# Zero products on TensorE ahead of the first scores

## The chip, the cores and the metric

The kernel runs on one core of a Trainium2 chip. A core has five engines that run side by side and meet through semaphores: TensorE (PE, matrix products; its weight loads are listed as PEld), VectorE (DVE), ScalarE (ACT), GpSimdE (POOL) and SyncE (SP), which only issues loads and stores to the DMA engines. The metric is the device time of one execution in microseconds (us), the median of several runs. A profile is one execution; its times count from the start of the span.

## The reference

Two layers follow each other. The first is attention with a window of 32 positions on either side, for 8 batch entries, 8 heads, 576 positions and 64 elements per head:

```python
scores = scale * np.matmul(q, k.transpose(0, 1, 3, 2))
mask = np.abs(pos[:, None] - pos[None, :]) <= window
attn = np.exp(scores - scores.max(-1)) / sum        # masked scores count as zero
attn_out = np.matmul(attn, v)                       # to x: [8, 576, 512]
```

The second is a causal attention with 4 experts, each position weighted over its best two:

```python
logits = x @ w_gate                                 # 4 experts
for e in range(4):
    q, k, v = x @ wq[e], x @ wk[e], x @ wv[e]       # 64 wide
    ye = causal_softmax(scale * q @ k.T) @ v @ wo[e]
    out += gate[e] * ye                             # gate: softmax over the best two, else 0
```

Inputs and outputs are float32.

## The kernel before

**Tiling.** The work goes through the 8 batch entries. In the first layer each entry has two groups of four heads. `sc(b, g, half, ...)` makes the scores of one group and one half of the queries: 80 products in the profile's count, 32 rows by 64 columns of the array each, in float32. Two such steps fill the four PSUM tiles `PS[0]` to `PS[3]` (each 128 partitions by two halves of 512 float32 elements). `ex` takes the exponential on ACT, `mk` multiplies by the mask on POOL or DVE, `av` multiplies by v on PE, `un` normalises on DVE, `xt`, `xf` and `xb` turn the result into the layout of the second layer. Its steps (`ga` to `gu` for the gate, `pp`, `pv` for projections, `ps` for scores, `po` for the product with v, `py` for the output) are woven in between.

**What sets the order.** `ORDER` is a list written out by hand, one word per step; `name@banks` says which PSUM halves the step uses. The loop at the end of the kernel runs through the list once and emits each step's instructions, so that every engine has its instructions in the list's order, and each waits by semaphore for what it needs. The dependencies come from the tile framework. All engine calls also go through a recording wrapper, `Watched`, whose `note` compares the boxes of two accesses and declares them independent if no box is common. All engine instructions therefore have line 146 in the profile. For PSUM tiles the wrapper's `boxes` widens each access to all 128 partitions and to whole halves of a tile.

```python
if b.tensor.name.startswith("PS"):
    p0, n, lo, hi = 0, 128, 2 * lo // row, (2 * hi - 1) // row + 1
    row = 2
```

**The head of the program.** The first words of the list are `fk01 fq01 fk11 s_pads fk00 s_warm gq01 s_ones fq10 fq00 fq11 gk00 ...`, and after them the first score steps, `sc001`, `sc000`, `sc011`, `sc010` (batch entry, group, half).
- `fk` and `fq` issue the first loads of k and q, half a group each, on the queues of SP and ACT.
- `gk` and `gq` transpose what has arrived from `kn`, `qn` into `Tkn`, `Tqn`, on DVE, two instructions each. `tk` and `tq` are the same for a whole group, later.
- `s_pads` clears the padding of eleven tiles and WG, on DVE. `s_ones` clears 2 x 32 columns of each half of each PSUM tile in partitions 64 to 127 (one instruction per tile), so that what the score products don't write is defined, and sets the ones next to v. `s_warm` loads ACT's table.
- `load`, used for all further loads, makes a load wait for the latest product emitted so far (`PACE`), so that loads follow the work.

```python
for t in PS:
    nc.vector.memset(t[64:128, :, 0:512].rearrange("p a (c x) -> p a c x", x=256)[:, :, :, 0:32], 0.0)
for t in VSB:
    nc.vector.memset(t[:, :, :, 64:66], 1.0)
```

DVE's order in the head is thus: clears of `s_pads`, transposes of `gq01`, the four PSUM clears and two clears of V, then the transposes of `gk00`, `gk01` and the others.

## Time and profile before

| What | Value |
|---|---|
| Time, median of 3 runs | 252.1 us (250.35 to 256.52) |
| Span of the profiled execution | 248.2 us |
| PE busy | 211.8 us (85% of the span) |
| DVE busy | 182.7 us (74%) |
| ACT busy | 151.3 us (61%) |
| POOL busy | 148.5 us (60%) |
| First product on PE | 10.77 us |
| Four score steps, in two pairs of 160 products | 10.77 to 15.23 us and 16.50 to 21.03 us |

The busy shares are averages over the whole span. The stretch that the change touches is the first 10 us, in which PE has nothing to do, and what follows from it. Lines of the timeline give start, time from start to end of a merged group, engine, line, operation, what is written and read, the count, and in brackets the idle time before it and what ended it. The clock that PE was granted (PEclk) is in tenths of full speed on the page and as a fraction in the table of stretches.

### The profile page before, as it was taken

How to read it: one execution, taken by the hardware profiler on the slowest of the kernel's cores; microseconds unless marked ns; L12 is line 12 of the kernel's file. 1: busy time of each engine (PE TensorE's matmuls, PEld its weight loads, DVE VectorE, ACT ScalarE, POOL GpSimd, SP SyncE). 2: the span in 40 equal slices, each digit the busy share in tenths (PEclk: the TensorE clock that was granted, in tenths of full speed). 3: DMA queues.
4: the chain of work that ended last, by engine and by line, in shares of the span. 5: the costliest groups of instructions: out<-in, count | busy, mean ns of one | idle time of the engine just before them, and what ended most of it. 6: DMA issues, size and time to landing. Idle time of an engine off the chain costs nothing.

```text
span 248.2 us, 12156 instructions
## 1 busy us (share of the span) xinstructions
PE 211.8 (85%) x5453; PEld 170.8 (69%) x5466; DVE 182.7 (74%) x373; ACT 151.3 (61%) x230; POOL 148.5 (60%) x164
## 2 busy tenths in 40 slices
PE   0277787999999869999579994999999999999981
PEld 0276774787879648886449864788789777887550
DVE  7986958699888967887827792889686654727770
ACT  2037656488678557768444782666674868492952
POOL 6038779338994997449971696048959488240310
PEclk9999997999999999999979998899999999999997
DMA  6968849676878995779975788034890061656045
GB/s 235 300 180 231 192 110 257 170 212 216 190 206 240 192 231 133 203 218 210 246 230 156 199 191 193 22 100 132 163 222 15 16 186 41 54 194 222 13 184 211
DMA packets 64787, 42.93 MB, mean 173 GB/s; under 512 B 54752, under 2 KB 55776, under 8 KB 64736
## 3 DMA queue, kind: packets, MB, share of 16 engines
q1 hardware_dynamic: 64080, 40.91, 64.7%
q10 hardware_dynamic: 656, 1.25, 1.4%
q8 instruction: 43, 0.70, 1.2%
q14 instruction: 8, 0.07, 0.1%
HBM read 30.42 MB, written 9.44 MB: 161 GB/s over the span
## 4 chain that ended last, share of the span: by engine, by line
PE 70%; DMA 12%; DVE 9%; issue 3%; ACT 3%; SPq 1%; ACTq 0%; DVEq 0%
PE PS L146 70%; DMA OTT<-OE 8%; DMA kn<-in_k_dram 2%; DVE XTB L146 2%; DMA V<-in_v_dram 1%; DVE Tkn L146 1%; ACT ATE L146 1%; DVE PS L146 1%; ACT Y L146 1%; DVE OE L146 1%; DVE Y L146 1%; ACT A L146 1%; DVE XTF L146 0%; DVE m L146 0%; ACT V L146 0%
## 5 line engine op out<-in xcount | busy, mean ns | idle before, releaser
L146 POOL TENSOR_TENSOR A<-A,MASKP 128x576 f32<-128x576 f32 x62 | 87.0, 1425 | 39.1 <-ACT A L146 39.1
L146 ACT ACTIVATE ATE<-PS 128x1024 bf16<-128x1024 f32 (+1 forms) x64 | 51.0, 835 | 23.6 <-PE PS L146 20.6
L146 PE MATMUL PS<-Tqn,Tkn 32*64 32x128 f32 (+2 forms) x2560 | 47.2, 276 | 15.8 <-DVE Tqn L146 11.3
L146 ACT ACTIVATE A<-PS 128x576 f32<-128x576 f32 x64 | 38.6, 650 | 34.2 <-PE PS L146 28.2
L146 PEld LDWEIGHTS PS<-Tqn,Tkn 32*64 32x64 f32 x2560 | 41.6, 141 | 21.6 <-DVE Tqn L146 11.7
L146 POOL TENSOR_SCALAR_AFFINE_SELECT ATE<-ATE 128x512 bf16<-128x512 bf16 (+1 forms) x48 | 24.7, 528 | 29.7 <-ACT ATE L146 29.6
L146 PE MATMUL PS<-V,A 128*64 128x65 f32 (+1 forms) x1280 | 40.9, 228 | 1.3 <-ACT V L146 0.8
L146 PEld LDWEIGHTS PS<-V,A 128*64 128x64 f32 (+1 forms) x1280 | 37.7, 137 | 5.1 <-issue 2.6
L146 DVE STREAM_TRANSPOSE Tkn<-kn 128x576 f32<-128x576 f32 (+1 forms) x36 | 37.3, 1122 | 3.9 <-DMA kn<-in_k_dram 2.6
L146 DVE STREAM_TRANSPOSE Tqn<-qn 128x576 f32<-128x576 f32 (+1 forms) x36 | 37.3, 1120 | 2.1 <-DMA qn<-in_q_dram 2.1
L146 PE MATMUL PS<-WO,OTT 128*128 128x512 bf16 (+1 forms) x83 | 18.9, 345 | 11.5 <-DMA OTT<-OE 9.2
L146 DVE TENSOR_TENSOR XN<-PS,RC 128x512 f32<-128x512 f32 (+1 forms) x40 | 25.5, 638 | 1.4
L146 POOL COPY V<-V 64x1024 f32<-64x1024 f32 (+1 forms) x22 | 21.8, 992 | 5.3 <-issue 2.5
L146 ACT COPY Y<-PS 128x1024 f32<-128x1024 f32 (+1 forms) x18 | 15.0, 842 | 14.6 <-PE PS L146 10.7
L146 PE MATMUL PS<-XTB,WQ 128*128 128x288 bf16 x128 | 19.5, 304 | 1.8 <-DVE XTB L146 1.8
L146 PE MATMUL PS<-ident,XN 128*128 128x128 f32 x144 | 19.2, 277 | 0.7 <-issue 0.7
L146 POOL CAST XTB<-XTF 128x128 bf16<-128x128 f32 (+1 forms) x18 | 11.4, 647 | 13.6 <-ACT XTF L146 12.9
L146 PE MATMUL PS<-WV,XTB 128*128 128x256 bf16 (+1 forms) x192 | 18.6, 256 | 0.8 <-ACT A L146 0.4
L146 ACT COPY XTF<-PS 128x1024 f32<-128x1024 f32 (+1 forms) x26 | 16.5, 679 | 4.4 <-PE PS L146 3.7
L146 PE MATMUL PS<-XTB,WK 128*128 128x288 bf16 x128 | 18.9, 296 | 0.0
L146 PEld LDWEIGHTS <-OTT 128*128 128x128 bf16 (+1 forms) x96 | 6.9, 101 | 17.2 <-DMA OTT<-OE 9.7
L146 PEld LDWEIGHTS <-ATE 128*128 128x128 bf16 x480 | 16.5, 97 | 2.0 <-issue 0.8
(62 smaller groups left out, 247.7 us busy)
## 6 DMA issues: line engine op xcount, KB each, us to landing
V<-in_v_dram SPq DMA_DIRECT2D x32, 256.0 KB, 4.0
out_dram<-Y SPq DMA_DIRECT2D x16, 512.0 KB, 3.1
kn<-in_k_dram SPq DMA_DIRECT2D x14, 576.0 KB, 5.1
qn<-in_q_dram SPq DMA_DIRECT2D x14, 576.0 KB, 5.1
kn<-in_k_dram SPq DMA_DIRECT2D x4, 288.0 KB, 5.2
qn<-in_q_dram ACTq DMA_DIRECT2D x4, 288.0 KB, 5.6
V<-in_v_dram SPq DMA_DIRECT2D x8, 128.0 KB, 4.7
out_dram<-Y SPq DMA_DIRECT2D x15, 64.0 KB, 2.0
```

What stands on the lines that cost most here:

```text
L146: return lambda *a, **k: self._w.note(self._e, f(*a, **k))
```

## The change

Ahead of everything, a small tile `WZ` of 128 x 224 bf16 zeros is cleared on DVE, and TensorE multiplies zeros by zeros 72 times into a part of `PS[3]` that nobody reads before it is written again (second half, columns 288 to 511). The products have no use but to keep TensorE occupied while the first loads are under way, so that its clock[...] is up when the first scores come. Everything else in the list stands as it was.

```diff
 ORDER = """
-    fk01 fq01 fk11 s_pads fk00 s_warm gq01 s_ones fq10 fq00 fq11 gk00 ...
+    s_wm fk01 fq01 fk11 s_pads fk00 s_warm gq01 s_ones fq10 fq00 fq11 gk00 ...
@@
+    WZ = sb.tile([128, 224], BF16, name="WZ")
@@
+    def s_wm():
+
+        for i in range(72):
+            nc.tensor.matmul(PS[3][:, 1, 288:512], WZ[:, 0:128], WZ, start=True, stop=True)
@@
     with tc.manual_schedule():
+        nc.vector.memset(WZ, 0.0)
         nc.vector.memset(RC[0], 0.0)
         for step in ORDER.split():
```

The products are emitted through `nc.tensor.matmul`, not through the kernel's `mm`, so they don't count as the latest product for `load`.

## The prediction

> **What bounds the kernel now.** I read the chain that ended last first. It gives TensorE (PE) 70% of the span, but that is an average over stages. So I asked for the same chain in the first 30 us, where the change sits (columns: start us, us, what):

> ```profile
> 0.81 0.40 SPq L350
> ...
> 1.72 6.09 DMA kn<-in_k_dram
> 7.82 0.02 issue
> 7.84 2.34 DVE Tkn L146 x4
> 10.18 0.55 DVE Tqn L146
> 10.73 0.04 issue
> 10.77 4.46 PE PS L146 x139
> ```

> The head is a load, then VectorE (DVE), then PE. The load ends at 7.8 us, five transposes on DVE take 2.9 us, and only then can the first scores start. PE is empty until 10.77 us, but PE is not what is short there. The timeline of DVE and PE over the head and, in its last row, later (start us, us, engine, line, operation, count):

> ```profile
> 0.88 0.07 DVE L146 MEMSET RC<- 128x8 f32 x1 [0.88 <-PEq L672]
> ...
> 6.66 0.59 DVE L146 MEMSET PS<- 64x128 f32 x4
> 7.27 0.31 DVE L146 MEMSET V<- 128x128 f32 x2
> 7.84 2.34 DVE L146 STREAM_TRANSPOSE Tkn<-kn 128x288 f32<-128x288 f32 x4 [0.27 <-DMA kn<-in_k_dram]
> ...
> 10.77 4.45 PE L146 MATMUL PS<-Tqn,Tkn 32*64 32x64 f32 x160 [10.77 <-DVE Tqn L146]
> ...
> 16.50 4.53 PE L146 MATMUL PS<-Tqn,Tkn 32*64 32x64 f32 x176 [1.28 <-ACT A L146]
> ...
> 53.18 2.43 PE L146 MATMUL PS<-Tqn,Tkn 32*64 32x64 f32 x160
> ```

> DVE has 0.27 us of slack before the first k transpose; it is otherwise busy from 0.88 to 17.7 us without a break. And the same 160 score products take 4.45 us at 10.77 but 2.43 us at 53.18: the first four score steps run at half the clock. The page's clock row says 9 there, because the record begins with the first change it saw, near 20 us; the pace of the products is the witness. That is the 2 us per pair that the change is after.

> When the clock falls again is seen in stretches that I cut around idle times (stretch, length, busy times and counts of the engines, PEclk, DMA share, GB/s):

> ```profile
> 40.40:44.00 3.60, 3.55 (x16) 2.29 (x16) 2.94 (x13) 0.84 (x3) 3.40 (x3) 0.53 0.92 298
> 44.00:46.00 2.00, 2.00 (x18) 1.52 (x16) 1.61 (x2) 0.64 (x1) 1.44 (x2) 1.00 0.01 5
> 89.70:91.70 2.00, 0.00 (x0) 0.11 (x2) 1.24 (x3) 0.43 (x1) 2.00 (x2) 1.00 0.71 206
> 91.70:95.20 3.50, 3.45 (x96) 2.63 (x96) 2.15 (x3) 2.19 (x4) 2.34 (x3) 1.00 0.21 78
> 122.40:125.40 3.00, 0.00 (x0) 0.11 (x2) 0.55 (x1) 0.07 (x1) 2.33 (x3) 1.00 1.26 210
> 125.40:129.20 3.80, 3.75 (x44) 2.08 (x47) 0.76 (x1) 1.89 (x3) 2.78 (x3) 0.57 0.82 286
> 149.80:153.10 3.30, 0.06 (x2) 0.00 (x0) 1.18 (x3) 0.47 (x1) 3.01 (x4) 1.00 1.07 142
> 153.10:156.60 3.50, 3.40 (x62) 3.41 (x64) 0.90 (x2) 0.37 (x1) 0.00 (x0) 0.52 0.41 143
> ```

> An idle PE of 2.0 us keeps the clock; idle times of 3.0 and 3.3 us are each followed by about 3.4 us at half speed.

> [...] half-speed spells last 3.4 us and end in busy stretches. [...] products with N = 288 start every 240 ns cold and 121 ns warm, those with N = 256 every 108 ns. [...]

> **The change, part by part.**

> A `memset` of WZ (128 x 112 words) goes first on DVE. By the rows of XTB (two of 128 x 128 words in 0.31 us) it takes about 0.15 us. It delays the other clears by that, and 0.27 us of slack before the k transposes swallows it.

> The 72 products start at about 0.88 + 0.15 + 0.05 = 1.1 us on an empty PE. N is 224. Cold, 224 x 240/288 = 187 ns each; warm, 121 - 64 x (121 - 108)/32 = 95 ns by the trace's slope[...]. Their weight loads (98 ns warm, 152 cold in the rows of N = 288) lie under the products. [...]
> - Early release: 18 cold products (3.4 us) and 54 warm (5.2 us) end at 9.7 us.
> - Late release: 36 cold (6.8 us) and 36 warm (3.5 us) end at 11.4 us.
> - Middle: 10.5 us.

> If this were all, the stretch would end just as the first scores begin (10.77 us), warm.

> But it adds a wait. The products write the second half of the last PSUM tile, PS[3], columns 288 to 511. `s_ones` later clears columns 0 to 31 and 256 to 287 of each PSUM half. No element is shared, but the helper that declares independence, `Watched.boxes`, rounds every PSUM access to whole halves of a tile, so the clear of PS[3] is held to clash. In the built order of the changed kernel, DVE's fourth PSUM clear waits for a PE count of 72, which the last product alone raises. Queued behind it on DVE are the two clears of V, then all the transposes of q and k; the first scores wait for the first five of those. That clear ran at 7.09 us (the last 0.165 us of the 0.59). Now it runs when product 72 is complete: 10.5 + 0.17 (rest of its 0.26 us) + 0.05 = 10.75 us, between 9.9 and 11.6. Then 0.17 + 0.31 us of clears, and the k transposes start at 11.2 us instead of 7.84: **+3.4 us** (2.6 to 4.3). The scores start at 11.2 + 2.93 = 14.2 us.

> Does the warm clock pay it back? Between the last product and the first score PE idles 0.05 + 0.48 + 2.93 = 3.5 us, longer than both idle times above after which the clock fell. So the usual outcome is a clock that is back at half before the first score, and the four score steps run as slowly as now. The loads paced by products (`load`) move along with PE; those not paced (k and V issued by 7.83 us) land earlier against the work, for which I give 0.3 us back. Nothing downstream is anchored to anything else: scores, exponentials, masks and later loads all hang on these transposes. Sum: 252.1 + 3.4 - 0.3 = **255.2 us**.

> **The rivals.**
> - *The clock survives the gap* (18%). [...] Then both score pairs take about 2.4 us, 4.1 us less PE time. But DVE's own chain stays late: the second pair needs the second group's transposes, done at 15.5 us now and 18.9 us then. What comes back is bounded by DVE's 1.41 us wait for q before 19.14 us: about 1.7 of the 3.4. 252.1 + 1.7 = 253.8 us.
> - *Zeros never release the clock* (10%). 72 x 187 ns end at 14.6 us, the clear runs at 14.8, the transposes start at 15.3: +7.4, 259.5 us. [...] no row of this trace shows zero operands.
> - *Faster* (8%): the stretch is warm from its start, 72 x 96 ns end at 8.0 us, the wait costs 1.2 us, and the scores give back 4.1: 249.2 us. Against it: PE is cold at 10.77 us now after doing nothing.
> - *As worked out* (64%).

> **How the numbers follow.** The likeliest case gives 255.2. The three times before span 250.35 to 256.52, and full or half clock after later idle times (three further falls within the span, 1.7 us each at most) is drawn anew, so each case carries about 1.5 us either way. From 252.0 (below the surviving clock, less noise) to 259.0 us (main case at its late end, 256.1, plus noise, and short of the middle of the zero case) leaves out about 2 in 10. Slower by over 2% means above 257.1 us: nearly all of the zero case and a tenth or more of the main one, 0.19. Faster by over 2% (below 247.0 us) needs the fast case with luck, 0.03. Within 2%: 0.78.

> **What would show it.** The fourth PSUM clear on DVE should wait on PE until about 10.7 us, with the k transposes right after at 11.2; if it runs near 7 us, my wait is wrong. Starts of the 72 products should go from 187 to about 96 ns apart between 4.5 and 7.9 us; 187 to the end is the zero case. First scores at 13.3 to 15.1 us, the first 160 in about 4.4 us; if in 2.4, the clock survived. A first score near 10.8 us would overturn the forecast, as would a head late by 3.4 us whose lateness is gone by 60 us.

## The result, and the profile after

The changed kernel takes 267.6 us (265.2 to 272.8) beside 251.2 us of the kernel before (four runs each): a ratio of 1.073, 95% interval 1.051 to 1.095. The forecast was 255.2 us, at most 259.0; it had the direction and missed most of the size. The time of the kernel before spreads from 242 to 258 us over all its runs, so everything below is compared by ratios to runs of it made beside each kernel, and a ratio takes only those runs of a kernel that lie within 1.5% of its fastest (times are medians of all). The profile below is of the execution of 272.8 us.

The timeline of the head, after the change (start us, us, engine, line, operation, count, and in brackets what ended the idle time before it):

```profile
1.11 9.93 PE L146 MATMUL PS<-WZ 128*128 128x224 bf16 x72 [1.11 <-DVE RC L146]
...
6.78 0.45 DVE L146 MEMSET PS<- 64x128 f32 x3
...
11.15 0.17 DVE L146 MEMSET PS<- 64x128 f32 x1 [3.92 <-PE PS L146]
...
11.56 2.27 DVE L146 STREAM_TRANSPOSE Tkn<-kn 128x288 f32<-128x288 f32 x4
...
14.42 3.81 PE L146 MATMUL PS<-Tqn,Tkn 32*64 32x64 f32 x160 [3.38 <-DVE Tqn L146]
...
19.51 1.96 PE L146 MATMUL PS<-Tqn,Tkn 32*64 32x64 f32 x119 [1.28 <-ACT A L146]
...
24.16 3.24 PE L146 MATMUL PS<-Tqn,Tkn 32*64 32x128 f32 x121 [2.69 <-issue]
```

So far this is the forecast: the fourth PSUM clear waits for product 72, and the first scores start at 14.42 us, 3.65 us late. The last row is new. PE stops for 2.69 us in the middle of a row of score products that wait for nothing, and goes on with the same work. "issue" says that the profile shows no releaser. The chain that ended last has more of these (start us, us, what):

```profile
19.51 1.96 PE PS L146 x85
21.47 2.69 issue
24.16 1.30 PE PS L146 x30
...
28.43 3.20 PE PS L146 x112
31.63 2.69 issue
34.32 8.05 PE PS L146 x182
```

Over the whole span, PE's waits put down to issue (us in total, times, longest) were, before:

```profile
PE PS L146 <- issue: 4.1, 6, 1.2
```

and are after the change:

```profile
PE PS L146 <- issue: 22.7, 16, 3.6
```

The 18.6 us between them, with the 3.65 us of the head, come near the 22.8 us by which the two profiled spans differ (248.2 and 271.0 us). That the sum fits so well is luck: PE's other products also took 5.2 us longer (226.9 us busy, 9.9 of it on zeros, beside 211.8), and its other idle time was 4.6 us shorter. Part of the longer work goes with the pauses too: in each of the four longest (from 21.47, 31.63, 60.33 and 110.73 us, 2.7 to 3.6 us each) or within 1.1 us of its end the clock falls to half, at 24.09, 34.33, 65.05 and 112.83 us by the trace's clock record.

What does PE wait for? The pauses of 0.7 us and more without a semaphore begin after PE's record number 705, 1217, 1729, 2497, 3009, 4289, 4801, 5313, 6081 and 7873, with products, weight loads and the few waits of PE's own (45) counted together: always 193 plus a multiple of 256. The other six of the 16 waits for issue stand at such places as well. And the page lists a DMA queue that brings instructions (packets, MB, share of 16 engines):

```profile
q8 instruction: 43, 0.70, 1.1%
```

0.70 MB in 43 packets is 16 KB each, and 43 x 256 is 11,008, about PE's 11,076 products and weight loads. By these counts a packet is a block of 256 PE instructions. In the trace's packet records the one of the pause at 21.47 us lands at 22.72 and PE goes on at 24.15; the one of the pause before 63.96 us lands at 62.69. In the ten pauses listed above PE goes on 1.2 to 1.6 us after its packet has landed, and it enters none of the 42 blocks from record 450 on sooner than that. The packet itself takes 1.0 us (median of the 43; 0.9 to 1.9). Of the 43, 40 start 0.5 us or more after PE has entered the block before, the latest 4.4 us after. Together 0.5, 1.0 and 1.2 us make 2.7, so by this estimate a block that PE runs through in less than that, and often one of 4 or 5 us, can end with PE out of instructions; in the ten pauses 3.7 to 6.7 us passed from entering the block before to going on. Score products are the quickest work of the kernel before: 160 with their 160 weight loads take 2.43 us, which makes 1.9 us for a block.

The 22.7 us of waits stand at 16 of these 42 block edges. The first theory after the result was therefore: the 72 products are 144 instructions, 0.56 of a block; they move every later block edge by 144 instructions, perhaps into places where PE runs fast and loads are dense. The rivals: a late head that snowballs (loads, clock and engines out of step), or the number of instructions itself.

### The profile page after: what moved, and what is told of

Its sections match the earlier page's. It is cut to its first block, busy times and chain, and to the rows that moved or that the text cites. A ratio compares the mean times of both kernels' runs of the same rounds, so it can differ in the third digit from the quotient of the medians.

```text
span 271.0 us, 12314 instructions
## 1 busy us (share of the span) xinstructions
PE 226.9 (84%) x5538; PEld 180.8 (67%) x5538; DVE 184.2 (68%) x374; ACT 151.8 (56%) x230; POOL 148.0 (55%) x164
## 4 chain that ended last, share of the span: by engine, by line
PE 69%; DVE 9%; issue 9%; DMA 7%; ACT 3%; SPq 1%; ACTq 0%; DVEq 0%
PE PS L146 69%; DMA OTT<-OE 7%; DVE XTB L146 2%; DVE PS L146 1%; DVE Tqn L146 1%; ACT ATE L146 1%; DVE Tkn L146 1%; ACT Y L146 1%; DVE OE L146 1%; ACT A L146 1%; SPq L234 1%; DVE Y L146 1%; ACT V L146 1%; DVE XTF L146 0%; DVE m L146 0%
## 5 line engine op out<-in xcount | busy, mean ns | idle before, releaser
L146 POOL TENSOR_TENSOR A<-A,MASKP 128x576 f32<-128x576 f32 x62 | 86.9, 1426 | 57.9 <-ACT A L146 57.9
L146 ACT ACTIVATE A<-PS 128x576 f32<-128x576 f32 x64 | 38.6, 649 | 56.8 <-PE PS L146 51.8
L146 PE MATMUL PS<-Tqn,Tkn 32*64 32x128 f32 (+2 forms) x2560 | 48.5, 274 | 25.0 <-issue 20.1
L146 ACT ACTIVATE ATE<-PS 128x1024 bf16<-128x1024 f32 (+1 forms) x64 | 50.9, 835 | 25.7 <-PE PS L146 25.0
L146 PEld LDWEIGHTS PS<-Tqn,Tkn 32*64 32x64 f32 x2560 | 41.8, 139 | 32.0 <-issue 24.6
L146 POOL TENSOR_SCALAR_AFFINE_SELECT ATE<-ATE 128x512 bf16<-128x512 bf16 (+1 forms) x48 | 25.3, 541 | 34.3 <-ACT ATE L146 33.6
L146 PE MATMUL PS<-V,A 128*64 128x65 f32 (+1 forms) x1280 | 39.9, 223 | 1.8 <-issue 0.9
L146 DVE STREAM_TRANSPOSE Tqn<-qn 128x576 f32<-128x576 f32 (+1 forms) x36 | 37.3, 1118 | 5.2 <-DMA qn<-in_q_dram 5.2
L146 DVE STREAM_TRANSPOSE Tkn<-kn 128x576 f32<-128x576 f32 (+1 forms) x36 | 37.1, 1116 | 4.7 <-DMA kn<-in_k_dram 3.3
L146 PEld LDWEIGHTS PS<-V,A 128*64 128x64 f32 (+1 forms) x1280 | 36.4, 132 | 5.7 <-issue 3.0
L146 PE MATMUL PS<-WO,OTT 128*128 128x512 bf16 (+1 forms) x96 | 21.0, 355 | 8.7 <-DMA OTT<-OE 6.9
L146 DVE TENSOR_TENSOR XN<-PS,RC 128x512 f32<-128x512 f32 (+1 forms) x40 | 25.5, 638 | 1.4
L146 POOL COPY V<-V 64x1024 f32<-64x1024 f32 (+1 forms) x22 | 21.9, 995 | 8.3 <-DMA V<-in_v_dram 4.0
L146 ACT COPY Y<-PS 128x1024 f32<-128x1024 f32 (+1 forms) x18 | 15.0, 841 | 12.5 <-PE PS L146 7.7
L146 PE MATMUL PS<-WV,XTB 128*128 128x256 bf16 (+1 forms) x192 | 20.5, 270 | 0.5 <-ACT A L146 0.4
L146 PE MATMUL PS<-ident,XN 128*128 128x128 f32 x144 | 20.6, 293 | 0.0
L146 PE MATMUL PS<-XTB,WK 128*128 128x288 bf16 x128 | 19.2, 296 | 1.2 <-issue 1.2
L146 PEld LDWEIGHTS <-XTB 128*128 128x128 bf16 (+1 forms) x192 | 15.7, 107 | 5.2 <-issue 2.5
L146 ACT COPY XTF<-PS 128x1024 f32<-128x1024 f32 (+1 forms) x26 | 16.5, 675 | 4.3 <-PE PS L146 3.4
L146 PE MATMUL PS<-XTB,WQ 128*128 128x288 bf16 x128 | 18.0, 286 | 0.7 <-DVE XTB L146 0.7
L146 PE MATMUL PS<-QKE 64*128 64x64 bf16 (+4 forms) x192 | 18.1, 285 | 0.6 <-issue 0.6
L146 PEld LDWEIGHTS <-ATE 128*128 128x128 bf16 x480 | 17.2, 99 | 2.1 <-issue 0.8
(65 smaller groups left out, 253.8 us busy)
```

The source lines that it names most:

```text
L146: return lambda *a, **k: self._w.note(self._e, f(*a, **k))
```

## The experiments

**Undo the shift, keep the wait.** 128 products are 256 instructions, one whole block, with the same number of columns in all.

```diff
-        for i in range(72):
-            nc.tensor.matmul(PS[3][:, 1, 288:512], WZ[:, 0:128], WZ, start=True, stop=True)
+        for i in range(128):
+            nc.tensor.matmul(PS[3][:, 1, 288:414], WZ[:, 0:128], WZ[:, 0:126], start=True, stop=True)
```

> 128 products of N = 126 in place of 72 of N = 224: the same number of columns (16128), and the clear of PS[3] still waits for the last product, but the products and their weight loads are now 256 PE instructions, one whole block of the instruction fetch, in place of 144. Theory A (the head's wait costs some 3.5 us, the rest of the loss is PE waiting for instruction blocks, because a shift of 144 moves every block edge): edges are back where they were in the program, so 254 to 257 us, PE idle put down to issue near the 4 us of before, not the 23 us of the change. Theory B (the late head snowballs: loads, clock and the other engines fall out of step): as the change, 265 to 269 us. Theory C (more and shorter zero products are worse for themselves): above 267 us.

Measured: 1.010, interval 1.004 to 1.016. More products, and the loss falls from 7.3% to 1.0%. The tile `WZ` is the same here, so that its place in memory isn't the cause either. Its head is as late as the forecast said; its timeline:

```profile
10.55 0.17 DVE L146 MEMSET PS<- 64x128 f32 x1 [3.33 <-PE PS L146]
...
13.83 4.44 PE L146 MATMUL PS<-Tqn,Tkn 32*64 32x64 f32 x160 [3.38 <-DVE Tqn L146]
```

and its waits for issue are nearer to the 4.1 us of before than to the 22.7 us of the change:

```profile
PE PS L146 <- issue: 6.6, 10, 1.6
```

**Undo the wait, keep the shift.** The clear of PS[3] is taken out of `s_ones` and put first on DVE; the products then wait for it, 0.17 us, and nothing on DVE waits for them.

```diff
-        for t in PS:
+        for t in PS[0:3]:
             nc.vector.memset(t[64:128, ...], 0.0)
@@
+        nc.vector.memset(PS[3][64:128, ...], 0.0)
         nc.vector.memset(WZ, 0.0)
@@
-            nc.tensor.matmul(PS[3][:, 1, 288:512], WZ[:, 0:128], WZ, start=True, stop=True)
+            nc.tensor.matmul(PS[3][:, 1, 288:496], WZ[:, 0:128], WZ[:, 0:208], start=True, stop=True)
```

> The clear of PS[3] goes first on DVE, so that nothing on DVE waits for the zero products; 72 products stay (N = 208, so that they end a little sooner), and so does the shift by 144 instructions. Theory A: only the 3.5 us of the head come back, or a little more for a warm start, 259 to 265 us, with about 20 us of PE idle put down to issue. Theory B (the wait and what follows from it is all of the loss): 246 to 252 us.

Measured: 1.068 (1.060 to 1.076), 264.4 us. The scores start on time and warm (151 products in 2.61 us, where the cold ones of the shift alone, below, took 3.64 us), and almost all of the loss stays. The timeline of PE shows where the warm start goes:

```profile
10.79 2.61 PE L146 MATMUL PS<-Tqn,Tkn 32*64 32x64 f32 x151 [0.76 <-DVE Tqn L146]
15.38 0.35 PE L146 MATMUL PS<-Tqn,Tkn 32*64 32x64 f32 x9 [1.98 <-issue]
```

After the 151 warm products come 1.98 us put down to issue: the pair ends at 15.7 us, later than the cold pair of before (15.2 us). Over the whole span the waits for issue stay near those of the change:

```profile
PE PS L146 <- issue: 18.2, 15, 2.7
```

**Undo both.** Clear first, and 128 products of N = 112.

> Both: clear of PS[3] first, and 128 products (N = 112), a whole block of 256 instructions. Theory A: no wait and no shifted edges, so the time of before or up to 3 us less, 247 to 252 us; it may be the best of all. Theory B: the same as the kernel with the clear first and 72 products. Theory C: slower than that by the cost of 56 more products, 1 us or more.

Measured: 1.001 (0.987 to 1.014). The loss is gone, and no gain can be measured. PE's timeline:

```profile
10.79 1.92 PE L146 MATMUL PS<-Tqn,Tkn 32*64 32x64 f32 x95 [0.29 <-DVE Tqn L146]
13.97 1.10 PE L146 MATMUL PS<-Tqn,Tkn 32*64 32x128 f32 x65 [1.26 <-issue]
```

and its waits for issue over the whole span:

```profile
PE PS L146 <- issue: 4.9, 7, 1.3
```

Again PE stops at a block edge within the pair, which ends at 15.1 us, 0.15 us ahead of the cold one of before. So an added whole block isn't free either. In the profiles before and after the change the first packet lands at 14.92 and 16.58 us and PE enters the block of record 450 at 17.88 and 17.89 us, so that the first 449 records needed none. Before, they reach into the second pair, and PE passes the edge in the first pair (record 193, at 13.24 us) without a pause. Here 256 of them are the zero products with their weight loads, so that the same place is record 449, where the first packet is needed; PE goes on at 13.97 us, after 1.26 us put down to issue.

**The shift alone.** 72 products of N = 8: the same 144 instructions in 2.08 us.

```diff
-            nc.tensor.matmul(PS[3][:, 1, 288:512], WZ[:, 0:128], WZ, start=True, stop=True)
+            nc.tensor.matmul(PS[3][:, 1, 288:296], WZ[:, 0:128], WZ[:, 0:8], start=True, stop=True)
```

> 72 products of N = 8 in place of N = 224: 144 more PE instructions, but they end by about 5 us, before DVE comes to the clear of PS[3] at 7.1 us, so that the wait costs nothing[...]. Theory A: the first scores near 10.8 us as before, but 259 to 265 us in all, because the block edges are shifted. Theory B (wait or clock do the harm): 250 to 253 us, as before.

Measured: 1.066 (1.059 to 1.074). The products are done at 3.2 us, the clear runs at its old time, the first score starts at 10.78 us, cold (151 in 3.64 us), and the kernel still loses 6.6%:

```profile
6.77 0.59 DVE L146 MEMSET PS<- 64x128 f32 x4
...
10.78 3.64 PE L146 MATMUL PS<-Tqn,Tkn 32*64 32x64 f32 x151 [7.58 <-DVE Tqn L146]
```

Its waits for issue are again many:

```profile
PE PS L146 <- issue: 15.0, 16, 2.9
```

This fits neither the wait nor the clock as the main cause.

**Shifts of other sizes.** The same with the clear first and 128, 16, 96 or 112 products of N = 8 (`range(72)` changed alone).

> Clear of PS[3] first and 128 products of N = 8: 256 more PE instructions, one whole block, no wait[...]. Theory A (block edges decide): the time of before, ratio 0.99 to 1.01. Theory D (any instructions ahead of the scores do harm, by number): slower than the kernel with 72 such products, above 265 us. Set beside the kernel with 128 products of N = 112 it also tells what the warm start is worth: 2 to 4 us if the clock is worth what the paces say, nothing if the block fetch and the loads eat it.

> The same with 16 products of N = 8: edges shifted by 32 instructions. A tally of the trace of before (for each shift, sum over all blocks of how far a block's run time falls short of 4 us, relative to no shift) gives 4.9 us for 32, 6.5 us for 144, 2.9 us for 192 and 1.6 us for 224; scaled to the 16.5 us that the shift by 144 cost, theory A expects a ratio of about 1.05 here (1.02 to 1.06). Theory D: 1.015, in proportion to the number of instructions.

> The same with 96 products of N = 8: edges shifted by 192 instructions. Theory A by the tally: about 1.03 (1.01 to 1.05), less than for 72 products although there are more. Theory D: 1.09.

> The same with 112 products of N = 8: edges shifted by 224 instructions. Theory A by the tally: about 1.015 (1.00 to 1.03), near before. Theory D: 1.10.

| Products | Shift, instructions | Tally, us | Ratio (interval) |
|---|---|---|---|
| 16 | 32 | +4.9 | 1.050 (1.028 to 1.073) |
| 72 (clear not moved) | 144 | +6.5 | 1.066 (1.059 to 1.074) |
| 96 | 192 | +2.9 | 1.030 (1.002 to 1.057) |
| 112 | 224 | +1.6 | 1.019 (0.984 to 1.055) |
| 128 | 256 = 0 | 0 | no interval; 250.8 us in 4 runs beside 246.6 us of before in 7 |

The number of instructions doesn't decide: 144 cost 6.6% and 192 cost 3.0%, with intervals that just miss each other, and 256 cost 1.0% or less in the two kernels of 128 longer products above. That 32 cost more than 192 or 224 is shown by the middle values only, since the intervals of these three overlap. The row of 128 settles nothing by its time (its lowest run is 245.3 us beside 242.7 of before), nor does it tell what the warm start is worth. The tally was worked out from the trace of before alone. Its 4 us is a value I chose from the pauses (3.7 to 6.7 us from entering a block to going on); other values give other sums, so only the order means anything. With all of PE's records counted, that trace gives 4.8, 5.2, 2.8 and 1.5 us in place of 4.9, 6.5, 2.9 and 1.6, and the same order with 3.5 or 4.5 us for the 4. That no shift is the best of all it also gives: the hand-written order has its quick stretches where the edges aren't. The profile of the 128 short products has fewer waits for issue than even the kernel before:

```profile
PE PS L146 <- issue: 3.5, 5, 1.6
```

**The shift undone on the way.** 72 short products in the head, and 56 more ahead of a later gate step, which fill up the block.

```diff
+    def s_re():
+        for i in range(56):
+            nc.tensor.matmul(PS[0][:, 0, 440:448], WZ[:, 0:128], WZ[:, 0:8], start=True, stop=True)
@@
-    ... ga0@0 ...
+    ... s_re ga0@0 ...
```

> Clear of PS[3] first and 72 products of N = 8 in the head, as before; 56 more such products stand ahead of the first gate step (near 37 us), into columns of PS[0] that nobody reads. From there on the shift is 256 instructions, a whole block, so that it is in force for the first 37 us only. Theory A: only the stalls of these 37 us and some 1.5 us for the 56 products stay, ratio 1.00 to 1.02. Theory B (a disturbed head snowballs through all that follows, whatever the edges do): about 1.066, as the kernel with 72 short products.

Measured: 1.015 (0.998 to 1.031); the 56 products ran at 41.4 to 42.9 us. The second has `s_re ga2@0` in place of `s_re ga0@0`:

> The same with the 56 products ahead of the third gate step (near 115 us). Against the kernel before, the one with 72 short products had lost 9.3 us of its 12.6 us by there in its profile. Theory A: about 9 us and some 1.5 us for the products, ratio 1.03 to 1.05, between the kernel with the early repair and the one with none. Theory B: 1.066 or more.

Measured: 1.019 (1.000 to 1.039), below what was expected and not told apart in time from the early repair. Both intervals lie below that of the kernel without repair (1.059 to 1.074). My place was off: the 56 products ran at 92.9 to 94.4 us, not 115, and by 93 us the kernel without repair had lost 4.8 us of its 12.6, which with 1.4 us for the products makes 1.025. Its profile is clearer than its time. PE's waits for issue up to 100 us and from there on, with the repair at 93 us:

```profile
PE PS L146 <- issue: 9.8, 10, 3.2
...
PE PS L146 <- issue: 1.5, 4, 0.5
```

and in the kernel with 72 short products and no repair, the same two stretches:

```profile
PE PS L146 <- issue: 6.9, 9, 2.0
...
PE PS L146 <- issue: 8.1, 7, 2.9
```

The pauses stop where the shift stops. Beside the same instructions of ACT in the profile before, the repaired kernel is 9.3 us late near 95 us and 9.6 at the end (the profiled execution took 259.5 us); the one without repair is 5.2 us late near 95 us and 12.6 at the end. A snowball would have rolled on.

**The wait alone.** 128 products of N = 126 with the clear first differ from the first experiment in the wait only.

> 128 products of N = 126 with the clear of PS[3] first: the kernel of the first experiment without its wait, and nothing else different. Theory A: the wait is worth 3 to 4 us, so a ratio of 0.99 to 1.005 beside the 1.0099 with the wait. If the warm start were worth the 4 us that the paces of the scores promise, 0.98 to 0.985. If the wait is hidden, 1.01.

Measured: 1.009 (1.000 to 1.019), the same as with the wait, as the case of a hidden wait had it. The first score starts at 11.15 us in place of 13.83, after DVE, whose first k transpose waited 0.54 us for its load, and nothing of the 2.7 us is seen in the time; with these intervals the wait is worth about 1% at most. Two profiles suggest where it goes: between the 128 short products, nothing waiting, and the 128 long ones with the wait, the lateness of the same instruction of ACT is 3.1 us in the first scores, 2.0 us at 80 us, and 1.1 us at the end. Two thirds of it was made up on the way in that pair. One pair of profiles, so this is seen, not settled.

## Why the prediction was wrong

**What held.** The wait through the PSUM half that `boxes` rounds to: the clear at 11.15 us, forecast 9.9 to 11.6. The pace of the products: 187 ns, then 96 ns. The release of the clock by zeros: 7.02 us, forecast 4.5 to 7.9; the rival of zeros that never release it is out. The first scores at 14.42 us, forecast 14.2. And the clock fell in the gap, at 13.85 us by the trace's clock record. The head was right to 0.4 us. (That the clock would rise after one or two spells of 3.4 us was the author's estimate from the half-speed spells of before, 40.59 to 44.00 us in its clock record; that a whole busy spell is needed was not shown. Of its figures, the 96 ns stand where the slope gave 95, the sum for the clear makes 10.72 us, not 10.75, and the trace has 122 and 109 ns where it read 121 and 108; nothing hangs on any of these.)

**What was too simple.** The clock came back at 17.26 us, so that not all four score steps ran as slowly as before: the first 160 products took 3.81 us, and the second pair ran at full clock until the pause (119 in 1.96 us). Nor does the length of an idle time alone tell whether the clock falls: the first line of the forecast's table of stretches (40.40 to 44.00 us at 0.53; the fall at 40.59) follows an idle time of 1.81 us, shorter than the 2.0 us that kept the clock.

**The step that failed** is this sentence: "Nothing downstream is anchored to anything else: scores, exponentials, masks and later loads all hang on these transposes." PE's instruction supply is anchored to something else, to the count of instructions since the start, in blocks of 256: the 16 waits for issue stand at record 193 plus a multiple of 256. The 72 products were costed by time alone, 1.1 to about 10.5 us on an empty PE; their 144 places in the stream were costed at nothing, without a reason given. The runs put 6.6 to 6.8% there (both kernels with the shift and without the wait) of the 7.3%, some 16.5 us, in place of zero. What remains for the wait is about 1% or less, not resolved from zero: 1.010 with the wait and 1.001 or 1.009 without it, edges in place. The 3.4 us that I gave it were right at the first score and, by these ratios, too much at the end.

**Where the sign could be seen.** The trace of before had three such pauses (1.2 us before 27.80, 0.7 before 35.29, 1.2 at 86.4 us), put down to issue, with no semaphore at the first instruction after them, and 512 and 2,560 records apart. I passed over them as noise of the stretch. The instruction queue stood on the page. No rival covered the case; the range ended at 259.0 us, with 10% on an event of 259.5 us whose cause was another.

**What the change was for,** a shorter time, was reached by no kernel here: with the wait and the shift both removed the scores run faster (their first 95 products in 1.92 us and the other 65 in 1.10, where before 160 took 4.45 us) and the kernel gains nothing that can be measured (1.001, 0.987 to 1.014). The first pair's 2 us go into one late block (1.26 us), which the added products themselves brought into it, and the step that waits for the transposes of q, which start at 19.95 us there and at 19.14 us before. A warm start from fewer and longer products was not tried.

**Open.** Why a packet starts late was not tried by itself. The DMA share was 0.96 and 1.00 in the pauses at 21.5 and 31.6 us, but 0.23 in the one at 110.7 us (window 110.60 to 114.00). What holds a packet up is not shown.

## What to carry to other kernels

Count instructions as well as time: here 72 products were 144 records of PE, the waits for issue after the change stood at multiples of 256 in the count (behind record 193), and a shift of 144 cost 6.6% where 256 cost 1.0% or less. So compare variants at equal remainder by 256, or pad to a whole block, before a difference is laid to anything else. Idle time of PE of 0.7 us and more that is put down to issue, without a semaphore and at distances of whole multiples of 256 in the count of instructions, ended 1.2 to 1.6 us after the landing of an instruction packet in the profile after the change; set the instruction packets beside it. And where a helper rounds accesses, look up in the built order who waits for the last instruction of an added group.
